# Attention front of a fused kernel: transposes by token halves, mixing by column halves, three runs of one TensorE tiling a step

## The chip, the cores and the metric

One Trainium2 chip, of which one NeuronCore is used. The metric is the device time of one execution in microseconds (us); lower is better. Three runs of the kernel before gave a median of 671.93 us (670.54 to 672.46).

## The reference, cut to what matters

Block-wise linear attention with decay feeds a mixer. With B = 4 batches, H = 8 heads, S = 768 tokens, 64 elements a head, C = 512 channels:

```python
for b in range(S // 64):                        # attention, per head
    qb, kb, vb = q[:, :, sl], k[:, :, sl], v[:, :, sl]
    intra = (qb @ kb^T * Dmask) @ vb            # Dmask: powers of lam below the diagonal
    inter = (qb * lam_pow) @ kv_state
    out[:, :, sl] = intra + inter
    kv_state = lam_block * kv_state + (kb * rev_pow)^T @ vb
x = out as (B, S, C)
h = x^T @ U @ V                                 # U: S x 32, V: 32 x S, per batch
u = x + h^T                                     # mixing along the tokens
y = u + relu(u @ w_ch1) @ w_ch2                 # w_ch1: 512 x 2048, w_ch2: 2048 x 512
```

## The kernel before, in words

The tokens of all batches are cut into 24 tiles of 128 tokens (`NS` = 24, six a batch, `NT` = 6). The work has three parts.

The **front** is a loop of 24 steps, whose pieces are written out by hand in the list `pieces` (L562 to L584); each engine does its instructions in the order in which the pieces issue them. Step s has, in this order:

- `prep(s+1)` (L360): the q and k of the next tile, four 128x128 transposes each on TensorE into one PSUM bank each, and a ScalarE copy of each bank (L358) to `qt` and `kt`; then the loads of later q and k are issued on SyncE's queue. `raw_pool` has 3 buffers for q and v, 4 for k.
- `scale(s+1)`: GpSimd multiplies `qt` with powers of lam (`qs`, L383), and k of the tile after that (`ks`, L372).
- `mix(done)` with done = s - 7 (L512): one matmul of a 128x128 block `v_hl` by `p_hl` (128x512) into one bank, and the VectorE addition to the tile `x_nat` (L518).
- `intra(s)` (L446): 16 products of masked scores and v on tiles of 128 rows x 64 columns; ScalarE copies the result from PSUM to `x_nat` (L459).
- `state(s)` (L411): 8 products of k and v on 128x64 tiles, and the VectorE update of `kv` (L426); then the load of a later v. The last tile of a batch (c = 5) has none.
- `turned`: ScalarE and GpSimd finish the split of an earlier u (L551, L552).
- `scores(s+1)` (L394): 8 products of k and q, on 64x128 tiles up to s = 6, and on 64x64 tiles (16 products) from s = 7.
- `inter(s+1)` (L431): 16 products of `qs` and `kv` on 64x64 tiles. The first tile of a batch has none.
- `masked(s+1)` (L405): VectorE multiplies scores and mask, two instructions (L409), into `sm`, which `intra(s+1)` reads.
- `turn(done)` (L523): four 128x128 transposes of the mixed tile on TensorE into one bank, the store of the tile to `u_d` on SyncE's queue (L535), and two VectorE instructions that split it (`ut` L537, `u_hl` L548). It is in the front for the first 16 tiles.

At the first step of a batch `low(b-1)` (L464) gives x^T U for the batch before, on 128x32 tiles, and `low_rows` (L477) splits it into the `p_hl` that `mix` uses; at some steps `aside` puts one or two VectorE instructions of the split of the first two w_ch1 blocks behind `masked` (from s = 12 ahead of it).

The **first product** (`hidden`, L719) is u @ w_ch1, by 128x512 matmuls in FP32R. Its first units have the last eight `turn`, the last `mix` and the last `low` between their matmuls, at places of the list `rest` (L788 to L802). The **second product** (`product`, L857) ends the kernel.

PSUM in the front: six tags, `pq`, `pk`, `pt`, `pu` of one bank and `pss`, `px` of two, one buffer each. `put` uses `pt`, `mix` `pu`, and `state` the bank of `pk`.

Of the kernel before, what the change touches and what calls it, by code (L numbers as in the profile page):

```python
# [14 lines left out]
P = 128  # L15
# [3 lines left out]
def kernel(  # L19
# [319 lines left out]
    def keep_busy(n):  # L339

        out = one_bank([P, C], "idle", "pq")
        for i in range(n):
            nc.tensor.matmul(out=out[:, 0:P], lhsT=blank, rhs=blank, start=True, stop=True)  # L343
# [3 lines left out]
    def turn_half(s, a0, name):  # L347

        ts, tag = (qts, ("pq", "pt")) if name == "q" else (kts, ("pk", "pu"))
        if a0 == 0:  # L350
            ts[s] = att.tile([P, HP, P], FP32, tag=name + "t", bufs=2, name=name + "t")
        n = HP // parts(s)
        pt = one_bank([P, n, P], "p" + name, tag[a0 > 0])
        for a in range(a0, a0 + n):
            nc.tensor.transpose(  # L355
                out=pt[:, a - a0, :], in_=raw[s, name][:, 2 * a : 2 * a + 2, :], identity=ident
            )
        nc.scalar.copy(ts[s][:, a0 : a0 + n, :], pt)  # L358

    def prep(s):  # L360
        for a0 in range(0, HP, HP // parts(s)):
            for name in "qk":
                turn_half(s, a0, name)
        st[s].update(qt=qts.pop(s), kt=kts.pop(s))
        for name in "qk":
            load_next(name)
# [27 lines left out]
    def scores(s):  # L394
        qt, kt = st[s]["qt"], st[s]["kt"]
        st[s]["pss"] = pss = two_banks("pss", "pss").rearrange("p x (a i) -> p x a i", a=HP)
        for a in range(HP):
            for x in range(2):
                for rows in half if s > NT else [slice(0, P)]:
                    nc.tensor.matmul(  # L400
                        out=pss[rows, x, a, :], lhsT=kt[half[x], a, rows],
                        rhs=qt[half[x], a, :], start=True, stop=True,
                    )
# [7 lines left out]
    def state(s):  # L411
        c = s % NT
        if c < NT - 1:
            ks, vr = st[s]["ks"], raw[s, "v"]
            pkv = one_bank([P, HP, D], "pkv", "pk")
# [48 lines left out]
    def low(b):  # L464

        tag = "pq" if b else "pu"
        pp = one_bank([P, P], "pp", tag) if b < B - 1 else bank([P, P], "pp", "b2")
# [7 lines left out]
        pps[b] = pp  # L475

    def low_rows(b):  # L477

        pp, t = pps.pop(b), tmp("p_h")[0:R]
        h, h2, l, l2 = (p_hl[g * R : (g + 1) * R] for g in range(G))  # L480
        own = [(slice(g * R, (g + 1) * R), slice(g * P, (g + 1) * P)) for g in range(G)]
        if b == 0:

            rows_f = tmp("p_f")[0:R]
            for rows, cols in own:
                nc.scalar.copy(rows_f[:, cols], pp[rows])
            own = [(slice(0, R), slice(0, C))]
            pp = rows_f
        for rows, cols in own:
            nc.vector.tensor_scalar(  # L490
                t[:, cols].bitcast(U32), pp[rows].bitcast(U32), HI, None, ALU.bitwise_and
            )

        def low_part():
            for rows, cols in own:
                nc.vector.tensor_tensor(
                    out=l[:, cols], in0=pp[rows], in1=t[:, cols], op=ALU.subtract
                )

        def spread():  # L500
            nc.scalar.copy(h, t)
            nc.scalar.copy(h2, t)

        def spread_low():
            nc.scalar.copy(l2, l.bitcast(FP32))
# [5 lines left out]

    def mix(s):  # L512
        b, c = divmod(s, NT)
        pu = one_bank([P, C], "pu", "pu") if s < NS - NT - 1 else bank([P, C], "pu", "b2")
        nc.tensor.matmul(  # L515
            out=pu, lhsT=v_hl[:, c * P : (c + 1) * P], rhs=p_hl, start=True, stop=True
        )
        nc.vector.tensor_tensor(out=xs[s], in0=pu, in1=xs[s], op=ALU.add)  # L518

    uhl, ud, turned = {}, {}, {}  # L520
    hl_at, d_at = [hl_pool], [d_pool]

    def turn(s):  # L523
# [6 lines left out]
        pt = one_bank([P, CT, P], "put", "pt") if g < FG else bank([P, CT, P], "put", "b1")  # L530
        for ct in range(CT):
            nc.tensor.transpose(  # L532
                out=pt[:, ct, :], in_=xs[s][:, ct * P : (ct + 1) * P], identity=ident
            )
        nc.sync.dma_start(out=u_d[s], in_=xs.pop(s))  # L535
        t = tmp("ut").rearrange("p (c n) -> p c n", n=P)
        nc.vector.tensor_scalar(t.bitcast(U32), pt.bitcast(U32), HI, None, ALU.bitwise_and)  # L537
        hi, low, diff = uhl[g][:, 0, :, cols], uhl[g][:, 1, :, cols], ud[g][:, :, cols]
        if g >= FG:

# [7 lines left out]
        nc.vector.tensor_tensor(out=low, in0=pt, in1=t, op=ALU.subtract)  # L548
# [6 lines left out]

        turned[s] = rest

    pieces = [("prep", 0), ("scale", 0), ("scores", 0), ("inter", 0), ("masked", 0)]  # L562
    for s in range(NS):
# [3 lines left out]
        step = [("prep", s + 1), ("scale", s + 1)] * more + [("fade", s)] * (c == 1)  # L567
        step += [("late", s - 1)] * (s in (NT, 3 * NT - 1))
        step += [("mix", done)] * (0 <= done < NS - NT - 1)
        step += [("low", b - 1)] * (c == 0 and b > 0)  # L570
        step += [("low_rows", b - 1)] * (c == 0 and b > 0)
# [6 lines left out]
        step += [("scores", s + 1)] * more  # L578
        step += [("aside", s)] * (s >= 2 * NT)
        step += [("inter", s + 1), ("masked", s + 1)] * more  # L580
        step += [("fade", s + 1)] * (more and c > 0)
        step += [("aside", s)] * (s < 2 * NT)
        step += [("turn", done)] * (done >= 0 and done // TG < FG)
# [3 lines left out]
    def load_next(name, engine=nc.sync):  # L587
# [7 lines left out]
        "low": low, "low_rows": low_rows, "next_of_low": next_of_low, "mix": mix, "turn": turn,  # L595
        "scale": scale, "turned": lambda s: turned.pop(s)(),
# [80 lines left out]
    make_identity(nc, ident)  # L677
    keep_busy(2)
    pl = one_bank([P, H], "pl", "pt")
# [99 lines left out]
    def run_units(units, side, every=lambda i: None):  # L779
# [10 lines left out]
        (0, 4, "turn", c0 - 2), (0, 6, "mix", c0 - 1), (0, 9, "low", b), (0, 14, "low_rows", b),  # L790
# [179 lines left out]
```

## Time and profile before

| | us |
|---|---|
| median of 3 runs | 671.93 |
| the profiled execution | 671.76 |
| its span, from the first to the last instruction | 669.9 |
| TensorE busy in the span | 663.9 (99%) |
| VectorE / ScalarE / GpSimd busy | 497.5 / 277.5 / 112.1 |
| front, to the start of the first matmul of the first product | 118.98 |

The page gives busy time by engine, the span in 40 slices, and the chain of work that ended last. Below it, groups of instructions by line and shape are a second view, and the timeline (start, length, engine, line, operation, how many) a third. TensorE's records overlap: a matmul's length includes its passage through the array, so a rate is read from starts and not from lengths. An FP32 product shows as two records, a transpose as one. `128*64` ahead of a shape is the tile of the array: rows by columns.

### The profile page before, as it was taken

The page shows a single profiled execution, that of the slowest core. Times are in us where ns is not written, and L with a number is a line of the kernel's source. Part 1 is how long each engine was busy: PE and PEld are TensorE (multiplying, and loading weights), DVE is VectorE, ACT ScalarE, POOL GpSimd, SP SyncE. Part 2 cuts the span into 40 slices and gives each one's busy share as a digit, 9 for nine tenths or more (in the row PEclk, how much of TensorE's full clock was granted, in tenths as well). Part 3 has the DMA queues.
Part 4 walks back from the last instruction along what each step waited for, and adds up shares of the span by engine and source line. Part 5 has one row for each costly group of instructions (what it writes and reads, how often), then busy time and mean ns, then how long its engine had stood idle before and what let it go on. Part 6 is the DMA issues. An engine that isn't in the chain of part 4 may idle for free.

```text
span 669.9 us, 13328 instructions
## 1 busy us (share of the span) xinstructions
PE 663.9 (99%) x5204; PEld 544.5 (81%) x5204; DVE 497.5 (74%) x873; ACT 277.5 (41%) x517; POOL 112.1 (17%) x92
## 2 busy tenths in 40 slices
PE   9999999999999999999999999999999999999997
PEld 8898989788888888888888888888888888888886
DVE  4689989877999777777797265787586775865864
ACT  4675866454655444444454122232322322322320
POOL 4455767240000000000000000030030300300300
PEclk9999999999999999999999999999999999999999
DMA  8999894354776655555577989854363353543421
GB/s 188 219 234 248 212 246 141 102 196 153 262 251 233 215 202 202 201 202 204 204 282 273 326 308 392 282 184 136 95 220 95 118 196 95 160 155 94 163 90 63
DMA packets 131776, 131.29 MB, mean 196 GB/s; under 512 B 81346, under 2 KB 89794, under 8 KB 131714
## 3 DMA queue, kind: packets, MB, share of 16 engines
q1 hardware_dynamic: 130512, 130.05, 61.1%
q8 instruction: 41, 0.67, 0.4%
q10 hardware_dynamic: 1202, 0.39, 0.2%
q14 instruction: 21, 0.17, 0.1%
HBM read 80.09 MB, written 50.33 MB: 195 GB/s over the span
## 4 chain that ended last, share of the span: by engine, by line
PE 97%; DVE 1%; DMA 1%; ACT 0%; issue 0%; DVEq 0%; ACTq 0%
PE pz L733 27%; PE pz L868 13%; PE pz L866 13%; PE pd L743 13%; PE pd L870 13%; PE px L453 4%; PE pss L400 3%; PE put L532 2%; PE pq L355 2%; PE pkv L418 1%; PE pk L355 1%; PE px L441 1%; DMA qraw<-in_q_dram 1%; PE pp L470 1%; PE pu L515 1%; PE idle L343 0%
## 5 line engine op out<-in xcount | busy, mean ns | idle before, releaser
L733 PE MATMUL pz<-u_hl,w 128*128 128x512 f32 x768 | 190.5, 397 | 0.0
L733 PEld LDWEIGHTS pz<-u_hl,w 128*128 128x128 f32 x768 | 144.0, 188 | 35.4 <-issue 0.4
L868 PE MATMUL pz<-w_hl,m 128*128 128x512 f32 x384 | 151.1, 396 | 0.0
L866 PE MATMUL pz<-w_hl,m 128*128 128x512 f32 x384 | 150.9, 396 | 0.0
L870 PE MATMUL pd<-w_d,m 128*128 128x512 f32 x384 | 149.5, 396 | 0.0
L849 ACT ACTIVATE m<-mt 128x512 fp32r<-128x512 f32 x96 | 60.5, 632 | 196.4 <-PE pd L870 140.9
L850 DVE SCALAR_TENSOR_TENSOR m<-rm,m 128x512 fp32r<-128x512 f32 x96 | 71.4, 746 | 53.8 <-ACT m L849 53.5
L895 POOL TENSOR_TENSOR o<-o,u 128x512 f32<-128x512 f32 x20 | 29.9, 1527 | 447.4 <-DVE o L891 447.4
L748 DVE SCALAR_TENSOR_TENSOR r<-pd,r 128x512 f32<-128x512 f32 x96 | 61.8, 686 | 53.6 <-ACT r L739 43.5
L743 PE MATMUL pd<-u_d,w 128*128 128x512 f32 x384 | 98.6, 397 | 0.0
L739 ACT ACTIVATE r<-pz 128x512 f32<-128x512 f32 x96 | 52.2, 596 | 93.2 <-PE pz L733 92.5
L868 PEld LDWEIGHTS pz<-w_hl,m 128*128 128x128 f32 x384 | 72.3, 188 | 17.7
L870 PEld LDWEIGHTS pd<-w_d,m 128*128 128x128 f32 x384 | 72.3, 188 | 17.6
L866 PEld LDWEIGHTS pz<-w_hl,m 128*128 128x128 f32 x384 | 72.3, 188 | 17.6
L743 PEld LDWEIGHTS pd<-u_d,w 128*128 128x128 f32 x384 | 72.1, 188 | 17.3
L851 DVE SCALAR_TENSOR_TENSOR m<-m 128x512 fp32r<-128x512 f32 x96 | 69.1, 721 | 0.9
L848 DVE TENSOR_SCALAR mt<-rm 128x512 uint32<-128x512 uint32 x96 | 46.1, 481 | 26.4 <-DMA rm<-r_d 26.1
L409 DVE TENSOR_TENSOR sm<-pss,mask 128x512 f32<-128x512 f32 x48 | 30.9, 685 | 7.3 <-PE pss L400 7.1
L212 ACT CAST w<-wt 128x512 fp32r<-128x512 f32 x32 | 19.9, 620 | 30.6 <-DVE wt L209 23.4
L383 POOL TENSOR_TENSOR qs<-qt,powq 128x512 f32<-128x512 f32 x20 | 25.9, 1297 | 20.3 <-ACT qt L358 19.8
L453 PEld LDWEIGHTS px<-vraw,sm 128*64 128x64 f32 x768 | 24.6, 137 | 5.5 <-issue 2.3
L453 PE MATMUL px<-vraw,sm 128*64 128x64 f32 x768 | 28.1, 225 | 0.1
(88 smaller groups left out, 682.1 us busy)
## 6 DMA issues: line engine op xcount, KB each, us to landing
r_d<-r SPq DMA_DIRECT2D x96, 256.0 KB, 2.4
rm<-r_d SPq DMA_DIRECT2D x96, 256.0 KB, 2.7
words<-in_moe_w_ch_dram SPq DMA_DIRECT2D x30, 512.0 KB, 4.5
w_d<-w SPq DMA_DIRECT2D x16, 768.0 KB, 3.3
w_hl<-w_d SPq DMA_DIRECT2D x16, 512.0 KB, 6.3
vraw<-in_v_dram SPq DMA_DIRECT2D x24, 256.0 KB, 5.0
u_d<-x_nat SPq DMA_DIRECT2D x24, 256.0 KB, 3.7
u<-u_d SPq DMA_DIRECT2D x24, 256.0 KB, 4.0
```

The costliest lines, as they stand in the source:

```text
L453: nc.tensor.matmul(out=px[half[t], x, a, :], lhsT=sm[:, x, a, half[t]], rhs=vr[:, 2 * a + x, :], start=(first and a == 0), stop=(a == HP - 1),
L733: nc.tensor.matmul(out=acc[g][0], lhsT=w[:, n, ct, :], rhs=uhl[g][:, n, ct, :], start=(ct == 0 and n == 0), stop=(ct == CT - 1 and n == 1),)
L739: nc.scalar.mul(rs[g], acc[g][0], 4096.0 + 1.0)
L743: nc.tensor.matmul(out=acc[g][1], lhsT=w[:, 2, ct, :], rhs=ud[g][:, ct, :], start=(ct == 0), stop=(ct == CT - 1),)
L748: nc.vector.scalar_tensor_tensor(rs[g], acc[g][1], 4096.0, rs[g], ALU.mult, ALU.add)
L848: nc.vector.tensor_scalar(t.bitcast(U32), r.bitcast(U32), HI, None, ALU.bitwise_and)
L849: nc.scalar.activation(out=m[:, 0], in_=t, func=AF.Relu)
L850: nc.vector.scalar_tensor_tensor(m[:, 1], r, 0.0, hi, ALU.max, ALU.subtract)
L851: nc.vector.scalar_tensor_tensor(m[:, 2], hi, E, low, ALU.mult, ALU.subtract)
L866: nc.tensor.matmul(out=pz, lhsT=m[:, 0, cols], rhs=hl[:, 0], start=first, stop=False)
L868: nc.tensor.matmul(out=pz, lhsT=m[:, 1, cols], rhs=hl[:, 1], start=False, stop=end)
L870: nc.tensor.matmul(out=pd, lhsT=m[:, 2, cols], rhs=dd, start=first, stop=end)
```

## The change

The six tags become four of two banks each: `pm`, `pss`, `pqk`, `px`. q and k are transposed together into `pqk` by halves of the tokens: 16 transposes of 64 rows to 128x64, each half to a bank of its own. `turn` does the same with 8 transposes into the first half of `pm`'s banks, and `mix` computes halves of the columns with 64 of the 128 rows each, in 4 matmuls of 128x256, into the second half of these banks. `state` takes a bank of `pqk`, `low` one of `px`. Scores are on 64x64 tiles from the second tile on.

In a step the order is now `prep(s+1)`, `turn(done-1)`, `mix(done)`, then `intra(s)` and `state(s)`, then `scores(s+1)` and `inter(s+1)`. The VectorE instructions of `turn` and `mix` are pieces of their own (`split`, `mixed`), ahead of `intra`; the store of the tile is one too, at the end of the step. `low(b)` stands at the end of a batch's last step, and ScalarE copies its result from PSUM. `mix` of tile 17 moves from the first product to step 23. As the changed program's waits stand, the copies of q and k both wait for the last transpose of k, and `split` waits for the last matmul of `mix`.

```diff
@@ -338,29 +338,36 @@
 
     def keep_busy(n):
 
-        out = one_bank([P, C], "idle", "pq")
+        out = two_banks("idle", "pm")[:, 0]
         for i in range(n):
             nc.tensor.matmul(out=out[:, 0:P], lhsT=blank, rhs=blank, start=True, stop=True)
 
     qts, kts = {}, {}
 
-    def turn_half(s, a0, name):
-
-        ts, tag = (qts, ("pq", "pt")) if name == "q" else (kts, ("pk", "pu"))
+    def turn_parts(s, a0):
+
+        n = HP // parts(s)
         if a0 == 0:
-            ts[s] = att.tile([P, HP, P], FP32, tag=name + "t", bufs=2, name=name + "t")
-        n = HP // parts(s)
-        pt = one_bank([P, n, P], "p" + name, tag[a0 > 0])
-        for a in range(a0, a0 + n):
-            nc.tensor.transpose(
-                out=pt[:, a - a0, :], in_=raw[s, name][:, 2 * a : 2 * a + 2, :], identity=ident
-            )
-        nc.scalar.copy(ts[s][:, a0 : a0 + n, :], pt)
+            for ts, name in ((qts, "qt"), (kts, "kt")):
+                ts[s] = att.tile([P, HP, P], FP32, tag=name, bufs=2, name=name)
+        pt = two_banks("pqk", "px" if a0 else "pqk")[:, :, 0 : 2 * n * D]
+        pt = pt.rearrange("p t (n a i) -> p t n a i", n=2, a=n)
+        for i, name in enumerate("qk"):
+            for a in range(n):
+                for t in range(2):
+                    nc.tensor.transpose(
+                        out=pt[:, t, i, a, :],
+                        in_=raw[s, name][half[t], 2 * (a0 + a) : 2 * (a0 + a) + 2, :],
+                        identity=ident[half[t], half[t]],
+                    )
+        for i, ts in enumerate((qts, kts)):
+            nc.scalar.copy(
+                ts[s][:, a0 : a0 + n, :].rearrange("p a (t i) -> p t a i", t=2), pt[:, :, i]
+            )
 
     def prep(s):
         for a0 in range(0, HP, HP // parts(s)):
-            for name in "qk":
-                turn_half(s, a0, name)
+            turn_parts(s, a0)
         st[s].update(qt=qts.pop(s), kt=kts.pop(s))
         for name in "qk":
             load_next(name)
@@ -396,7 +403,7 @@
         st[s]["pss"] = pss = two_banks("pss", "pss").rearrange("p x (a i) -> p x a i", a=HP)
         for a in range(HP):
             for x in range(2):
-                for rows in half if s > NT else [slice(0, P)]:
+                for rows in half if s > 0 else [slice(0, P)]:
                     nc.tensor.matmul(
                         out=pss[rows, x, a, :], lhsT=kt[half[x], a, rows],
                         rhs=qt[half[x], a, :], start=True, stop=True,
@@ -412,7 +419,7 @@
         c = s % NT
         if c < NT - 1:
             ks, vr = st[s]["ks"], raw[s, "v"]
-            pkv = one_bank([P, HP, D], "pkv", "pk")
+            pkv = two_banks("pkv", "pqk")[:, 0, 0 : HP * D].rearrange("p (a e) -> p a e", a=HP)
             for a in range(HP):
                 for x in range(2):
                     nc.tensor.matmul(
@@ -463,8 +470,7 @@
 
     def low(b):
 
-        tag = "pq" if b else "pu"
-        pp = one_bank([P, P], "pp", tag) if b < B - 1 else bank([P, P], "pp", "b2")
+        pp = two_banks("pp", "px")[:, 0, 0:P] if b < B - 1 else bank([P, P], "pp", "b2")
         for c in range(NT):
             for g in range(G):
                 nc.tensor.matmul(
@@ -472,53 +478,100 @@
                     rhs=xs[b * NT + c][:, g * P : (g + 1) * P],
                     start=(c == 0), stop=(c == NT - 1),
                 )
-        pps[b] = pp
+        if b == B - 1:
+            pps[b] = pp
+            return
+        pps[b] = rows_f = tmp("p_f")[0:R]
+        for g in range(G):
+            nc.scalar.copy(rows_f[:, g * P : (g + 1) * P], pp[g * R : (g + 1) * R])
 
     def low_rows(b):
...
+        rows_f = pp
+        nc.vector.tensor_scalar(t.bitcast(U32), rows_f.bitcast(U32), HI, None, ALU.bitwise_and)
+        wide = [slice(x * 2 * P, (x + 1) * 2 * P) for x in range(2)]
+
+        def place(g, low):
+            return p_hl[g * R : (g + 1) * R, wide[low]]
+
+        def spread():
+            for g in range(G):
+                nc.scalar.copy(place(g, 0), t[:, wide[g // 2]])
...
     def next_of_low(b):
         pps[b].pop(0)()
 
+    pms = {}
+
+    def both_halves(s):
+        if s not in pms:
+            pms[s] = two_banks("pm", "pqk" if s == NS - NT - 1 else "pm")
+        return pms[s]
+
     def mix(s):
         b, c = divmod(s, NT)
-        pu = one_bank([P, C], "pu", "pu") if s < NS - NT - 1 else bank([P, C], "pu", "b2")
-        nc.tensor.matmul(
-            out=pu, lhsT=v_hl[:, c * P : (c + 1) * P], rhs=p_hl, start=True, stop=True
-        )
+        weights = v_hl[:, c * P : (c + 1) * P]
+        if b < B - 1:
+            pm = both_halves(s)[:, :, 2 * P :]
+            for low in range(2):
+                for x in range(2):
+                    nc.tensor.matmul(
+                        out=pm[:, x], lhsT=weights[half[x]],
+                        rhs=p_hl[half[x], low * 2 * P : (low + 1) * 2 * P],
+                        start=(low == 0), stop=(low == 1),
+                    )
+            return
+        pu = bank([P, C], "pu", "b2")
+        nc.tensor.matmul(out=pu, lhsT=weights, rhs=p_hl, start=True, stop=True)
         nc.vector.tensor_tensor(out=xs[s], in0=pu, in1=xs[s], op=ALU.add)
+
+    def mixed(s):
+        pm, x = pms.pop(s)[:, :, 2 * P :], xs[s].rearrange("p (x e) -> p x e", x=2)
+        nc.vector.tensor_tensor(out=x, in0=pm, in1=x, op=ALU.add)
 
     uhl, ud, turned = {}, {}, {}
     hl_at, d_at = [hl_pool], [d_pool]
+
+    def store(s):
+        nc.sync.dma_start(out=u_d[s], in_=xs[s])
 
     def turn(s):
 
@@ -527,16 +580,17 @@
             uhl[g] = hl_at[g >= FG].tile([P, 2, CT, N], F32R, tag="hl", name="u_hl")
             ud[g] = d_at[g >= FG].tile([P, CT, N], F32R, tag="d", name="u_d")
         cols = slice(n * P, (n + 1) * P)
-        pt = one_bank([P, CT, P], "put", "pt") if g < FG else bank([P, CT, P], "put", "b1")
-        for ct in range(CT):
-            nc.tensor.transpose(
-                out=pt[:, ct, :], in_=xs[s][:, ct * P : (ct + 1) * P], identity=ident
-            )
-        nc.sync.dma_start(out=u_d[s], in_=xs.pop(s))
-        t = tmp("ut").rearrange("p (c n) -> p c n", n=P)
-        nc.vector.tensor_scalar(t.bitcast(U32), pt.bitcast(U32), HI, None, ALU.bitwise_and)
         hi, low, diff = uhl[g][:, 0, :, cols], uhl[g][:, 1, :, cols], ud[g][:, :, cols]
         if g >= FG:
+            pt = bank([P, CT, P], "put", "b1")
+            for ct in range(CT):
+                nc.tensor.transpose(
+                    out=pt[:, ct, :], in_=xs[s][:, ct * P : (ct + 1) * P], identity=ident
+                )
+            store(s)
+            del xs[s]
+            t = tmp("ut").rearrange("p (c n) -> p c n", n=P)
+            nc.vector.tensor_scalar(t.bitcast(U32), pt.bitcast(U32), HI, None, ALU.bitwise_and)
 
             nc.vector.scalar_tensor_tensor(diff, t, 1.0 + E, pt, ALU.mult, ALU.subtract)
             uf = tmp("uf").rearrange("p (c n) -> p c n", n=P)
@@ -545,7 +599,14 @@
             nc.gpsimd.tensor_tensor(out=low, in0=uf, in1=t, op=ALU.subtract)
             return
 
-        nc.vector.tensor_tensor(out=low, in0=pt, in1=t, op=ALU.subtract)
+        pt = both_halves(s + 1)[:, :, 0 : 2 * P].rearrange("p t (c i) -> p t c i", i=D)
+        for ct in range(CT):
+            for n in range(2):
+                nc.tensor.transpose(
+                    out=pt[:, n, ct, :], in_=xs[s][half[n], ct * P : (ct + 1) * P],
+                    identity=ident[half[n], half[n]],
+                )
+        del xs[s]
 
         def rest():
             nc.scalar.mul(hi, t, E)
@@ -553,22 +614,37 @@
                 out=diff, in0=hi.bitcast(FP32), in1=low.bitcast(FP32), op=ALU.subtract
             )
 
+        def parts_of(what):
+            return what.rearrange("p c (t i) -> p t c i", t=2)
+
+        t = tmp("ut").rearrange("p (c n) -> p c n", n=P)
+        split_t = parts_of(t.bitcast(U32))
         turned[s] = rest
 
-
-
-
+        def split():
+            nc.vector.tensor_scalar(split_t, pt.bitcast(U32), HI, None, ALU.bitwise_and)
+            nc.vector.tensor_tensor(
+                out=parts_of(low), in0=pt, in1=parts_of(t), op=ALU.subtract
+            )
+
+        splits[s] = split
+
+    splits = {}
 
     pieces = [("prep", 0), ("scale", 0), ("scores", 0), ("inter", 0), ("masked", 0)]
     for s in range(NS):
         b, c = divmod(s, NT)
         done = s - NT - 1
         more = s + 1 < NS
-        step = [("prep", s + 1), ("scale", s + 1)] * more + [("fade", s)] * (c == 1)
+        turns = done > 0 and (done - 1) // TG < FG
+        mixes = 0 <= done < NS - NT - 1
+        step = [("prep", s + 1), ("scale", s + 1)] * more
+        step += [("turn", done - 1)] * turns + [("mix", done)] * mixes
+        step += [("mix", done + 1)] * (not more)
+        step += [("fade", s)] * (c == 1)
         step += [("late", s - 1)] * (s in (NT, 3 * NT - 1))
-        step += [("mix", done)] * (0 <= done < NS - NT - 1)
-        step += [("low", b - 1)] * (c == 0 and b > 0)
-        step += [("low_rows", b - 1)] * (c == 0 and b > 0)
+        step += [("split", done - 1)] * turns + [("mixed", done)] * mixes
+        step += [("mixed", done + 1)] * (not more)
         step += [("intra", s)]
         step += [("next_of_low", b - 1)] * (c == 0 and b > 0)
         step += [("late", s)] * (s < NT - 1 or s == NT) + [("state", s)]
@@ -576,11 +652,13 @@
         step += [("turned", done - 1)] * (done > 0) + [("late", s)] * (done >= 0)
         step += [("next_of_low", b - 1)] * (c == 0 and b > 0)
         step += [("scores", s + 1)] * more
+        step += [("low", b)] * (more and c == NT - 1)
         step += [("aside", s)] * (s >= 2 * NT)
         step += [("inter", s + 1), ("masked", s + 1)] * more
+        step += [("low_rows", b)] * (more and c == NT - 1)
         step += [("fade", s + 1)] * (more and c > 0)
         step += [("aside", s)] * (s < 2 * NT)
-        step += [("turn", done)] * (done >= 0 and done // TG < FG)
+        step += [("store", done)] * (done >= 0 and done // TG < FG)
         pieces += step
     waiting = {name: list(range(NS)) for name in "qkv"}
 
@@ -593,6 +671,7 @@
         "prep": prep, "fade": fade, "scores": scores, "masked": masked, "inter": inter,
         "intra": intra, "state": state,
         "low": low, "low_rows": low_rows, "next_of_low": next_of_low, "mix": mix, "turn": turn,
+        "mixed": mixed, "store": store, "split": lambda s: splits.pop(s)(),
         "scale": scale, "turned": lambda s: turned.pop(s)(),
     }
     def v_steps():
@@ -675,8 +754,8 @@
     for name in "qkv":
         load_next(name)
     make_identity(nc, ident)
+    pl = two_banks("pl", "pss")[:, 0, 0:H]
     keep_busy(2)
-    pl = one_bank([P, H], "pl", "pt")
     nc.tensor.matmul(out=pl, lhsT=lam_row[:, H:], rhs=lam_row[:, 0:H], start=True, stop=True)
     keep_busy(3)
     nc.vector.tensor_copy(out=lamb, in_=pl)
@@ -787,7 +866,7 @@
     c0, b = NS - NT, B - 1
     rest = [
         (0, 4, "enter", None),
-        (0, 4, "turn", c0 - 2), (0, 6, "mix", c0 - 1), (0, 9, "low", b), (0, 14, "low_rows", b),
+        (0, 7, "turn", c0 - 2), (0, 9, "low", b), (0, 14, "low_rows", b),
         (0, 14, "next_of_low", b), (0, 14, "next_of_low", b), (0, 14, "next_of_low", b),
         (0, 18, "turn", c0 - 1), (0, 22, "mix", c0),
     ]
```

## Prediction

> **What bounds the kernel now.** I read the page first: the span and the chain of work that ended last.
>
> ```profile
> span 669.9 us, 13328 instructions
> ...
> PE 97%; DVE 1%; DMA 1%; ACT 0%; issue 0%; DVEq 0%; ACTq 0%
> ```
>
> TensorE (PE) is the chain. The change touches only the front, so next comes the timeline of TensorE in one of its steps.
>
> ```profile
> 48.35 0.66 PE L532 MATMUL put<-ident,x_nat 128*128 128x128 f32 x4
> 48.84 0.60 PE L355 MATMUL pq<-ident,qraw 128*128 128x128 f32 x4
> 49.28 0.60 PE L355 MATMUL pk<-ident,kraw 128*128 128x128 f32 x4
> 49.63 0.47 PE L515 MATMUL pu<-vp 128*128 128x512 f32 x1
> 50.04 1.15 PE L453 MATMUL px<-vraw,sm 128*64 128x64 f32 x32
> 51.02 0.64 PE L418 MATMUL pkv<-vraw,ks 128*64 128x64 f32 x16
> 51.59 1.10 PE L400 MATMUL pss<-qt,kt 64*64 64x128 f32 x32
> 52.51 0.64 PE L441 MATMUL px<-kv,qs 64*64 64x64 f32 x32
> ```
>
> Starts count here. The next step begins at 53.09, so a step is 4.74 us with no idle time in it: 12 transposes and the mix take 1.69 (48.35 to 50.04), intra 0.98, state 0.57, scores 0.92, inter 0.58. The tiling (the number pair ahead of the shape) changes three times. VectorE in the same step:
>
> ```profile
> 49.91 0.68 DVE L537 TENSOR_SCALAR ut<-put 128x512 uint32<-128x512 uint32 x1
> 50.62 0.69 DVE L548 TENSOR_TENSOR u_hl<-put,ut 128x512 fp32r<-128x512 f32 x1
> 51.23 0.68 DVE L518 TENSOR_TENSOR x_nat<-pu,x_nat 128x512 f32<-128x512 f32 x1
> 51.82 0.41 DVE L426 TENSOR_TENSOR kv<-pkv,faded 128x256 f32<-128x256 f32 x1
> 52.76 1.29 DVE L409 TENSOR_TENSOR sm<-pss,mask 128x512 f32<-128x512 f32 x2 [0.52 <-PE pss L400]
> ```
>
> From start to start ut costs 0.71, u_hl 0.61, x_nat 0.60, kv 0.35, sm 0.60 each: 3.5 us, and 0.4 to 0.8 of `aside`. VectorE is close behind TensorE. Last, SyncE's queue:
>
> ```profile
> 76.81 0.74 SPq L535 DMA_DIRECT2D u_d<-x_nat  x1
> 77.64 0.38 SPq L279 DMA_DIRECT2D qraw<-in_q_dram  x1
> 78.12 0.63 SPq L279 DMA_DIRECT2D kraw<-in_k_dram  x1
> 78.85 3.22 SPq L279 DMA_DIRECT2D vraw<-in_v_dram  x1
> 82.17 0.73 SPq L535 DMA_DIRECT2D u_d<-x_nat  x1
> ```
>
> The issues follow each other within 0.1 us, from 8 to 100 us, and the DMA share in steps of the front is 0.74 to 0.97. The buffer that the load at 78.85 fills (v of tile 17) was free when tile 14's state ended at 76.6, so the 3.22 us are no wait for TensorE: the queue runs at its own pace. **Loads and stores are a second bound that a faster TensorE does not move.**
>
> **What the Trainium skill says.** "TensorEngine Tiling (Array Packing)", Key Properties: a change of the tiling mode drains TensorE. The trace agrees: from the last transpose's start to the next tiling's first record it is 0.203 us where 0.109 is the pace, so about 0.09 a change. "TensorE: Matmul & The Clock Gate", Part 3: matmuls of different row groups run at once. The early scores agree: two 64x128 records start 7 ns apart, and each pair takes 0.109 like one 128x128 record. The same page, LDWEIGHTS: a load costs its columns divided by 1.2 GHz, 107 ns for 128, whatever the rows. For a transpose the trace differs: the first two loads of `put` start 57 ns apart (87.77 and 87.83). "PSUM — Partial Sum Buffer", bank collisions: no two engines on one bank and quadrant at a time. That fits the new waits: q's copy behind k's transposes, `split` behind the mix, as these share banks.
>
> **The change, part by part.**
>
> *Transposes.* A 128x128 transpose takes 0.109 (48.84 to 49.28 is four). In halves 64 columns stream instead of 128, and two row tiles run together: a pair should take what a pair of 128x64 records takes in intra, 0.058. The weight load of 0.057 fits under it. Unknown: such a transpose is not in the trace. Its bounds are 0.058 and 0.109 a pair (the page's 107 ns, or no concurrency); below 0.058 no row goes. I take 0.058. Twelve pairs, of which eleven intervals lie ahead of the mix: 11 x 0.051 = 0.56 us a step.
>
> *Mix.* Before: one matmul of 512 columns. After: two pairs of 256 columns, the same columns streamed, if FP32R keeps its rate at 256. I take 0; from -0.03 to +0.2 a step.
>
> *Changes of tiling.* Three before, three after: 0. Scores of steps with s up to 6 take 1.09 (15.44 to 16.53) on 64x128 tiles and 0.92 on 64x64: 0.16 saved in each early step, whose transposes save 8 x 0.051 = 0.41. Together 0.57.
>
> *The new wait on VectorE.* Let the transposes start at 0. The last pair starts at 0.70 (0.055 first load, 11 x 0.058), the last mix record about 0.92, intra at 1.13, and inter would start at 1.13 + 0.98 + 0.57 + 0.92 = 3.60. `split` can start 0.41 after the last mix record (0.31 of passage, 0.1 to the waiting engine, as kv starts 0.1 after pkv's end): 1.33. Behind it on VectorE stand ut 0.71, u_hl 0.61, x_nat 0.60, kv 0.42, and 0.06 to TensorE: kv is ready at 3.73, and inter, which reads it, waits 0.13. Before, ut followed `put`, which came first in the step, and had this time. Bounds: 0 (an earlier release) to 0.3. Queued behind the wait are kv and masked; masked starts after scores at 3.9, ends its second half at 5.1, and the next intra wants it at 5.5, so it is no later bound; with an `aside` of 0.6 ahead of it, 5.4, still in time.
>
> A full step is then 4.74 - 0.56 + 0.13 = 4.31: 0.43 saved. ScalarE's copies of q and k end at 1.9, ahead of state (2.1) which reuses their bank; GpSimd's qs ends at 2.7, ahead of 3.6. Its three instructions are 3.6 us.
>
> *The queue's cap.* A tile's v landed before it was read by: tile 4 0.2 us (26.86, intra at 27.07), tile 7 1.6 (38.79, 40.43), tile 17 4.65 (issue at 78.85, landing 6.0 later at 84.8, intra at 89.46). The store of tile 6 landed at 82.3, and ScalarE writes over its buffer at 85.9: 3.65, and 0.7 more before TensorE feels it. TensorE can be ahead by these amounts and no more, since the stores and loads keep their order and nothing of them is shortened. Early steps: 0.57 each from tile 4, capped at 1.6 by tile 7. Then ten steps of 0.43 would give 5.9 at tile 17; the cap leaves 4.65. After it the queue pulls away (tile 18 has 5.9, tile 21 6.5), and five full steps add 2.15: 6.8.
>
> *Moved pieces.* `mix` of tile 17 leaves the first product (0.235 saved there) and enters the last front step (0.22), which saves 0.2 of transposes. `low` keeps its 1.25 us; before, TensorE stood about 0.6 ahead of `put` at 61.7 for a late `x_nat`, and `turn` now comes a step after `mix`; against it the copies of `low`'s result, 4 x 0.26 on ScalarE, lie ahead of q's. I set these against each other, and keep +-0.5. Sum: 6.8 + 0.2 = 7.0 us. The first product follows at TensorE's pace, so all of it arrives at the end.
>
> The profiled execution's span goes from 669.9 to 662.9, its time (1.9 us more) from 671.76 to 664.8. The median is 0.2 above it: 664.9.
>
> **Rivals.**
>
> *Part of the gain (chance 0.12).* A pair at 0.080 instead of 0.058, or waits of 0.3 a step at inter and on ScalarE: about 0.2 a step over 15 steps and 1 us of the early ones, 4 us: 668. For it: VectorE is 88% to 98% busy in the steps from 68 us (4.18 to 4.76 of 4.7). Against: the sum above leaves 0.1 to 0.4 of slack.
>
> *The transposes do not get shorter (0.10).* Bound by the load of 128 columns, 0.109 a pair. Left are the early scores, at most 0.16 x 5 = 0.8, and the new wait, 0.13 x 14 = 1.8: +1.0, 672.9. For it: the page's price, and the first two loads of the early FP32 scores (128 columns) do start 0.109 apart. Against: the 57 ns of a transpose's load.
>
> *VectorE becomes the bound (0.08), slower.* Its three reads ut, u_hl and x_nat now have pieces of 64 elements and two banks, and stand between mix and kv. A step is the way from the last mix record over these to inter (2.81) and on through inter and the next transposes (1.5). Each 0.1 more on each read lengthens it by 0.3. With what early steps gain, it decides from 0.18 more each; at 0.3 more (0.9 instead of 0.6) a step is 5.2 us, +0.47 over 14 steps less 1.6: +5, 676.9. Against: ScalarE reads `px` in pieces of 64 over two banks in 0.58, like its plain reads (0.57).
>
> **How the numbers follow.** The forecast has 0.70. Its own range: a front 4.5 to 9.9 us shorter, by a wait of 0.3 to none and a cap that moves a microsecond or two: 662.0 to 667.4. A range for 8 in 10 takes in the partial gain: 661.9 to 670.0. A measurement tells 0.3% (2 us) from no change; faster by more is the forecast and the partial gain, 0.82; within it the unshortened transposes, 0.10; slower 0.08.
>
> **What would show it.** Right: 16 transposes of q and k in about 0.9 us, pairs 0.058 apart; the step 4.2 to 4.4 us; the idle time ahead of inter on kv about 0.1; stalls ahead of intra on v's landing near tiles 3, 4, 7 and 16 to 17; landings where they were; the first product starting near 112. Wrong: pairs at 0.109; ut, u_hl or x_nat longer than 0.75; or v landing earlier than before, which lifts the cap and with it the gain.

## The result and the profile after

The change makes the kernel slower by 0.7%. Times are medians; the last two columns are from the one profiled execution of each kernel. The last one sums the pauses of TensorE, each over 0.1 us, that no wait in the profile explains and that lie at the packet boundaries described below.

| kernel | us | ratio to before (95%) | first product starts | TensorE idle without a wait, front |
|---|---|---|---|---|
| before | 672.19 (670.54 to 672.46) | | 118.99 | 0 |
| after | 676.55 (676.29 to 677.47) | 1.0072 (1.0053 to 1.0092) | 125.01 | 7.2 |

The whole loss is in the front: 6.0 us at the start of the first product, 5.8 on the span (the profiled execution is the slowest of the four after, with a mean granted clock of 0.997 where the other three have 1.000, so it shows 1.4 us more than the medians). The page after, span and chain:

```profile
span 675.7 us, 14142 instructions
...
PE 96%; issue 1%; DVE 1%; DMA 1%; ACT 0%; ACTq 0%; DVEq 0%
```

TensorE is still the chain, yet 1% is now "issue": time in which it waited for nothing that the profile shows. Its timeline (start, length, engine, line, how many, idle time ahead) in a late step of the front, to lay beside the step of before:

```profile
102.97 0.40 PE L358 MATMUL pqk<-ident,qraw 64*128 64x64 f32 x6
104.08 0.28 PE L358 MATMUL pqk<-ident,qraw 64*128 64x64 f32 x2 [0.71 <-issue]
104.14 0.47 PE L358 MATMUL pqk<-ident,kraw 64*128 64x64 f32 x8
...
105.08 1.15 PE L460 MATMUL px<-vraw,sm 128*64 128x64 f32 x32
106.07 0.64 PE L425 MATMUL pkv<-vraw,ks 128*64 128x64 f32 x16
106.63 1.10 PE L407 MATMUL pss<-qt,kt 64*64 64x128 f32 x32
107.68 0.59 PE L448 MATMUL px<-kv,qs 64*64 64x64 f32 x25
109.05 0.34 PE L448 MATMUL px<-kv,qs 64*64 64x64 f32 x7 [0.78 <-issue]
```

Six transposes of q run, then TensorE stands for 0.71 us in the middle of eight like instructions, whose data are all there; then 25 of 32 products of inter, and 0.78 us. Intra (0.99) and state (0.56) are what they were. The two gaps are 127 matmul records apart. There are twelve gaps of this kind, 7.2 us in all, and none has a wait. Counted in recorded instructions of TensorE (matmuls, weight loads and semaphore instructions), all twelve are a multiple of 256 apart, within one.

VectorE's three reads of PSUM, which a rival of the prediction had longer (the two numbers behind the bar are busy time in us and mean ns of one, from 40 us on), after:

```profile
L625 DVE TENSOR_SCALAR ut<-pm 128x512 uint32<-128x512 uint32 x15 | 10.3, 686 | 5.3 <-PE pm L556 5.2
L568 DVE TENSOR_TENSOR x_nat<-pm,x_nat 128x512 f32<-128x512 f32 x15 | 10.2, 680 | 0.0
L626 DVE TENSOR_TENSOR u_hl<-pm,ut 128x512 fp32r<-128x512 f32 x14 | 9.7, 691 | 0.5
```

And before:

```profile
L537 DVE TENSOR_SCALAR ut<-put 128x512 uint32<-128x512 uint32 x15 | 10.2, 681 | 0.0
L518 DVE TENSOR_TENSOR x_nat<-pu,x_nat 128x512 f32<-128x512 f32 x16 | 10.9, 681 | 0.0
L548 DVE TENSOR_TENSOR u_hl<-put,ut 128x512 fp32r<-128x512 f32 x15 | 10.4, 692 | 0.5
```

They are unchanged. SyncE's queue, around the load of tile 17's v, which is the second line:

```profile
80.27 0.52 SPq L279 DMA_DIRECT2D kraw<-in_k_dram  x1
81.35 0.61 SPq L279 DMA_DIRECT2D vraw<-in_v_dram  x1
82.06 0.76 SPq L574 DMA_DIRECT2D u_d<-x_nat  x1
83.25 0.37 SPq L279 DMA_DIRECT2D qraw<-in_q_dram  x1
83.72 1.59 SPq L279 DMA_DIRECT2D kraw<-in_k_dram  x1
86.55 0.37 SPq L279 DMA_DIRECT2D vraw<-in_v_dram  x1
```

This load lands at 86.04, and intra reads it at 93.82: 7.8 us in hand (before 4.65). The queue even has pauses now (85.31 to 86.55). It waits for TensorE, and not TensorE for it.

**What ends a gap.** The page has a queue of its own for instructions; before and after:

```profile
q8 instruction: 41, 0.67, 0.4%
```

```profile
q8 instruction: 44, 0.72, 0.5%
```

0.72 MB in 44 packets is 16.4 KB each; over 5610 matmuls and 5610 weight loads it is 64 bytes an instruction, so a packet holds 256 instructions: 126 matmuls, 126 loads and a few others. Below, such a set of 256 is called a piece. Packets of this queue in the trace of after, beside the first record of the piece that they bring (us):

| packet | first record | gap ahead | record after packet's end |
|---|---|---|---|
| 50.01 to 50.97 | 52.34 | 1.94 | 1.4 |
| 74.66 to 75.60 | 76.95 | 0.83 | 1.4 |
| 96.92 to 97.86 | 99.19 | 0.48 | 1.3 |
| 101.80 to 102.67 | 104.08 | 0.71 | 1.4 |
| 106.57 to 107.45 | 109.05 | 0.78 | 1.6 |

At all twelve gaps TensorE resumes 1.26 to 1.60 us after the end of a packet. Before, packets ended mostly 1.7 to 3.1 us ahead of their first record. So the **theory**: TensorE runs short of instructions, as their supply is late. A full step has 140 matmul records now (before 125), to be issued in less time. "Runtime: NRT & Kernel Launch", Instruction fetch mechanics, of the Trainium skill describes refills in blocks of 256 instructions, fetched while the block before runs, and holds them mostly hidden. The trace agrees on the block, and not on the hiding: 7.2 us of gaps.

**Rivals**: VectorE's new wait, or loads that land too late, hold the step, and the gaps are only how the trace shows it. The next runs tell these apart.

### The profile page after: what moved, and what is told of

It reads as the page before. It is cut to its first block, busy times and chain, and to the rows that moved or that the text cites. A ratio compares the mean times of both kernels' runs of the same rounds, so it can differ in the third digit from the quotient of the medians.

```text
span 675.7 us, 14142 instructions
## 1 busy us (share of the span) xinstructions
PE 661.4 (98%) x5610; PEld 540.5 (80%) x5610; DVE 496.3 (73%) x864; ACT 281.6 (42%) x534; POOL 113.5 (17%) x92
## 4 chain that ended last, share of the span: by engine, by line
PE 96%; issue 1%; DVE 1%; DMA 1%; ACT 0%; ACTq 0%; DVEq 0%
PE pz L812 27%; PE pz L947 13%; PE pz L945 13%; PE pd L822 13%; PE pd L949 13%; PE px L460 4%; PE pss L407 4%; PE pqk L358 2%; PE px L448 2%; PE pkv L425 1%; PE pp L476 1%; PE pm L556 1%; PE pm L605 1%; DMA kraw<-in_k_dram 1%; PE put L587 1%
## 5 line engine op out<-in xcount | busy, mean ns | idle before, releaser
L460 PE MATMUL px<-vraw,sm 128*64 128x64 f32 x768 | 31.4, 228 | 2.8 <-issue 1.7
L460 PEld LDWEIGHTS px<-vraw,sm 128*64 128x64 f32 x768 | 26.3, 138 | 7.5 <-issue 2.4
```

The source lines that it names most:

```text
L460: nc.tensor.matmul(out=px[half[t], x, a, :], lhsT=sm[:, x, a, half[t]], rhs=vr[:, 2 * a + x, :], start=(first and a == 0), stop=(a == HP - 1),
```

## Experiments: more and fewer instructions, idle queues

**Scores on 64x128 tiles throughout** (8 products a step instead of 16, of two records each):

```diff
-                for rows in half if s > 0 else [slice(0, P)]:
+                for rows in [slice(0, P)]:
```

> The changed kernel with its scores on 64x128 tiles in every step: 124 matmul records a full step instead of 140 (an early one 112 instead of 128), each with its weight load, and 0.16 us more array time a step. Supply theory (TensorE gets its instructions in pieces of 256, one in about 4.85 us while the loads run, so 126 records with their loads cannot take less): the gaps inside runs of like records mostly go, a step takes about 4.75, the first product starts at 118 to 120 and the time is 669 to 673, faster than the change. VectorE theory (the new wait and longer reads hold a step): TensorE's own work is 0.16 longer in 22 steps and the time is 676 to 680. Load theory (q, k and v land too late): nothing moves, 676 to 677.

**After and before without most loads** (both leave out the loads of q, k and v of later tiles and compute with other data):

```diff
...
+        bufs = 4 if name == "k" else 3
+        if s >= bufs:
+            raw[s, name] = held[name, s % bufs]
+            return
...
-        raw[s, name] = t
+        raw[s, name] = held[name, s] = t
```

> The changed kernel without the loads of q, k and v after the first three tiles (four of k): later tiles read the buffers of earlier ones again, so the output is that of other data. TensorE's instructions are the same. Supply theory: a piece of instructions comes faster through idle queues, the gaps without a wait go, a full step takes 4.3 to 4.4, the first product starts at 111 to 114 and the time is 662 to 666. VectorE theory: the time stays at 675 to 677. Load theory: 662 to 667 as well, but then the gaps of the change must have been waits for a landing.

> The kernel before without the same loads (output of other data). Supply theory: its 125 records a step are within the supply, so little moves: first product at 117.5 to 119, time 670 to 672; beside the changed kernel without loads this gives what the change is worth where instructions are not short, 5 to 8 us. VectorE theory: the changed kernel without loads is slower than this one by about the 4 us that separate the kernels with loads. Load theory: as the supply theory.

**The kernel before with empty products**, at the head of `inter` (`none` is a tile of zeros):

```diff
...
+        if s > 0:
+            for i in range(16):
+                x, t = divmod(i % 4, 2)
+                nc.tensor.matmul(
+                    out=both[half[t], x, N - 1 : N], lhsT=none[half[x], half[t]],
+                    rhs=none[half[x], 0:1], start=True, stop=True,
+                )
```

> The kernel before with 16 empty products a step more (bf16, one column, on 64x64 tiles just ahead of inter, into an unused column): 141 matmul records a step with their loads. At inter's pace (32 records in 0.58 us) they are at most 0.29 us of work a step, 6.7 us over 23 steps. Supply theory: a full step grows to 141/126 x 4.85 = 5.4 while the loads run, early ones to about 4.6; gaps without a wait appear in the middle of runs, 126 records apart, and the time rises by 8 to 13 us, to 680 to 685. VectorE and load theories: no such gaps, and a rise of 2 to 7 us, 674 to 679.

| kernel | us | ratio to before (95%) | first product starts | idle without a wait |
|---|---|---|---|---|
| after, wide scores | 671.55 | 0.9981 (0.9970 to 0.9993) | 120.32 | 1.5 |
| after, no loads | 669.02 | 0.9941 (0.9921 to 0.9962) | 117.44 | 0.6 |
| before, no loads | 670.82 | 0.9978 (0.9965 to 0.9990) | 117.80 | 0 |
| before, 16 more | 677.00 | 1.0058 (1.0037 to 1.0079) | 123.34 | 0.4 |

Each set of experiments ran beside the kernel before, whose medians were 672.87 in this set, 671.59 in the second and 671.87 in the third. The ratios take this out; times of different sets can be off against each other by about 1 us.

Wide scores: more work for TensorE, fewer instructions, and 5 us less than after (6 by the ratios). Neither rival allows that. No loads: the same instructions, and the gaps are nearly gone (0.6 us left). The share of the DMA engines that the data queue takes between 10 and 110 us, after without loads, and after (9 to 109 us):

```profile
q1 hardware_dynamic: 7044, 5.87, 18.7%
```

```profile
q1 hardware_dynamic: 70827, 21.53, 88.7%
```

What did not come as expected tells more. Sixteen more products cost 4.1 us and not 8 to 13: undisturbed steps took 4.89 us, with 141 records and no gap. So the theory's fixed rate, a piece in 4.85 us, is wrong: here 126 records in 4.37 us were mostly served. The supply is a **latency**: in after, a packet starts 1.2 to 2.6 us (at the two worst gaps 3.4 and 3.6) after TensorE has begun the piece before, takes 0.9 to 1.5, and its first record runs at least 1.26 later. A gap comes where this is longer than the time in which TensorE spends 126 records, and that is 3.96 at the change's pace of 4.4 a step. The traces also show which part the loads lengthen. In the median a packet starts 2.0 us into the piece before with loads and 1.2 without, while the packet itself takes 0.96 and 0.99.

The change without loads gained 1.8 us on its partner, not 5 to 8, as its expectation had it: something else is missing from the forecast too (below).

**The threshold itself**: `range(32)` in place of `range(16)`.

> The kernel before with 32 empty products a step instead of 16: 157 records a full step. The first 16 made an undisturbed full step 0.15 us longer (4.74 to 4.89), so these make it 5.04, and 126 records then take 4.05 us as in the changed kernel, where 16 had left 4.37. Supply theory, as it now stands (a piece of instructions is asked for when TensorE begins the one before it, and needs 0.5 to 2.5 us in a queue, 0.9 to 1.5 of transfer and at least 1.3 to the first instruction, in sum 3.7 to 4.9): gaps without a wait as in the changed kernel, 0.2 to 0.8 at most boundaries, about 5 us, and the time is 683 to 688. If the gaps belong to something else in the change, only the work is added, 0.15 a step, 3.5 us on the 677.0 with 16: 680 to 681.

682.56 us, ratio 1.0155 (1.0134 to 1.0177), with no part of the change in it. A step is 5.11, so 126 records take 4.10, and the gaps are there, 3.2 us without a wait (16 more had 0.4), again in the middle of runs:

```profile
61.42 0.42 PE L439 MATMUL px<-none 64*64 64x1 bf16 x32
61.75 0.47 PE L449 MATMUL px<-kv,qs 64*64 64x64 f32 x17
63.50 0.46 PE L449 MATMUL px<-kv,qs 64*64 64x64 f32 x15 [1.28 <-issue]
```

It lies just under the range expected: the work grew by 0.22 a step instead of 0.15, but the gaps by 2.7 us instead of about 5, and the kernel before was 1.3 us faster in this set. The mechanism is shown on both kernels. Over the traces of all thirteen kernels of this document there are 58 such gaps in the front; they end 1.23 to 1.67 us after the end of a packet, and no piece begins less than 1.2 us after its packet. How many gaps there are depends on more than the rate.

## Experiments: why the change gains little even without gaps

Times from the start of one intra to a later one, in us, from the traces (undisturbed: without a gap):

| tiles (all of them counted) | before, no loads | after, no loads | after |
|---|---|---|---|
| 0 to 4 (early) | 21.76 | 21.36 | 22.07 |
| one early step, undisturbed | 4.29 | 4.05 | 4.05 |
| 5 and 6 (first end of a batch) | 9.09 | 10.38 | 10.68 |
| one full step, undisturbed | 4.74 | 4.42 | 4.53 |
| 11 and 12 (second end) | 10.80 | 10.03 | 10.03 |
| 17 and 18 (third end) | 10.13 | 10.53 | 11.27 |

A full step of after without loads:

```profile
74.04 1.15 PE L464 MATMUL px<-vraw,sm 128*64 128x64 f32 x32
75.02 0.64 PE L429 MATMUL pkv<-vraw,ks 128*64 128x64 f32 x16
75.59 1.20 PE L411 MATMUL pss<-qt,kt 64*64 64x128 f32 x32
76.65 0.69 PE L452 MATMUL px<-kv,qs 64*64 64x64 f32 x32
77.27 0.46 PE L362 MATMUL pqk<-ident,qraw 64*128 64x64 f32 x8
77.57 0.41 PE L362 MATMUL pqk<-ident,kraw 64*128 64x64 f32 x8
77.82 0.41 PE L609 MATMUL pm<-ident,x_nat 64*128 64x64 f32 x8
78.05 0.48 PE L560 MATMUL pm<-vp 64*128 64x256 f32 x4
78.46 0.73 PE L464 MATMUL px<-vraw,sm 128*64 128x64 f32 x14
```

Transposes and mix take 1.19 (77.27 to 78.46) instead of 1.69: the shorter transposes are real. From scores to inter it is 1.06 instead of 0.92; `kv` ends on VectorE at 76.50:

```profile
76.08 0.42 DVE L437 TENSOR_TENSOR kv<-pkv,faded 128x256 f32<-128x256 f32 x1
```

So inter waits 0.14 on VectorE, the wait that was forecast with 0.13.

The early steps fell from 4.29 to 4.05 only. My first idea was the way from scores over the mask to intra. So this run multiplies only half of it:

```diff
...
+            n = HP if s == 0 else HP // 2
             nc.vector.tensor_tensor(
-                out=sm[:, x], in0=pss[:, x], in1=mask[:, x], op=ALU.mult
+                out=sm[:, x, 0:n], in0=pss[:, x, 0:n], in1=mask[:, x, 0:n], op=ALU.mult
             )
```

> The changed kernel without loads, and with the mask multiplied into half of the scores' columns only (two VectorE instructions of 256 elements instead of 512; the other half keeps the first tile's values, so the output is of other data). TensorE's instructions are the same. Latency theory (an early step is the way from scores over both halves of sm to intra, and the shorter transposes only leave TensorE waiting there): early steps go from 4.05 to 3.7 to 3.8, full ones from 4.41 to about 4.35, the time from 669.0 to 665.5 to 667.5. If TensorE's own work or its supply sets the early steps, they stay at 4.05 and the time at 668.5 to 669.5.

667.17 us, in the range that the idea gave, but 1.3 of the gain comes from an earlier start in the profile (intra of tile 0 at 8.84 against 10.16); the early steps stayed at 4.05 and the full ones at 4.42. As the only cause the idea fell. The products of state in three early steps of this kernel, what they waited for:

```profile
its engine sat idle before it (us, times) until:
  PE pkv L434: 4.4, 3
  ACT kt L368: 0.8, 3
```

(The first line is VectorE, which reads the tile; the second counts weight loads as well as products, 0.14 us each.) State takes a bank of `pqk` and cannot start before ScalarE has copied k out of it: at 23.09 the copy ends, at 23.15 state starts, 0.14 after intra left TensorE free. With the full mask (after without loads) intra takes 1.30 instead of 0.98 (23.20 to 24.50), as the second half of `sm` ends at 23.52, and the copy of k ends at 24.44, just ahead of state. So two chains of the same length hold the early step; the runs with both taken away are below.

The first end of a batch, after without loads:

```profile
35.60 0.42 PE L362 MATMUL pqk<-ident,kraw 64*128 64x64 f32 x8
36.55 1.15 PE L464 MATMUL px<-vraw,sm 128*64 128x64 f32 x32 [0.54 <-ACT p_f L490]
...
39.68 0.69 PE L452 MATMUL px<-kv,qs 64*64 64x64 f32 x32 [0.26 <-DVE kv L435]
...
40.83 1.14 PE L560 MATMUL pm<-vp 64*128 64x256 f32 x4
41.90 0.28 PE L464 MATMUL px<-vraw,sm 128*64 128x64 f32 x2
```

Intra of tile 6 needs the bank in which `low` left its result, and waits for ScalarE's four copies; inter waits for `kv`; the first mix takes 1.07 instead of 0.42, as its `p_hl` is late. In all these waits are about 1.5 us.

## Experiments: taking these waits away

**`low` of batch 0 in a bank of `pm`, `aside` ahead of `low_rows`**, with 64x64 and with 64x128 scores:

```diff
-        pp = two_banks("pp", "px")[:, 0, 0:P] if b < B - 1 else bank([P, P], "pp", "b2")
+        pp = two_banks("pp", "px" if b else "pm")[:, 0, 0:P] if b < B - 1 else bank([P, P], "pp", "b2")
...
+        step += [("aside", s)] * (s == NT - 1)
         step += [("low_rows", b)] * (more and c == NT - 1)
...
-        step += [("aside", s)] * (s < 2 * NT)
+        step += [("aside", s)] * (s < 2 * NT and s != NT - 1)
```

> The changed kernel with low of the first batch in the bank of pm instead of px, and the VectorE instructions of aside ahead of low_rows in that step. The wait of 0.54 us ahead of intra of tile 6 (ScalarE's four copies of low's result) and the 0.26 on kv go, and the first mix waits less for p_hl. If these waits are a loss of their own: 0.8 to 1.4 us, 675.1 to 675.8. If the supply of instructions sets the pace there too: under 0.5, 676 to 676.7.

> The same edit on the changed kernel with 64x128 scores in every step, which had 671.6. There the supply is short in fewer places, so more of the 0.8 to 1.4 us should show: 670.2 to 671. If it beats the kernel before by more than its interval, it is faster than both.

| kernel | us | ratio to before (95%) | first product starts | idle without a wait |
|---|---|---|---|---|
| after, low moved | 674.99 | 1.0044 (1.0026 to 1.0061) | 122.54 | 5.3 |
| wide, low moved | 670.51 | 0.9981 (0.9971 to 0.9990) | 119.42 | 1.3 |

The first is 1.6 us faster than after, but the intervals of the two ratios overlap, and tiles 5 and 6 take 10.42 instead of 10.68, only 0.26 of it: the 0.54 at intra is gone, and state then waits 0.35. The rest fits the gaps, 5.3 us instead of 7.2. The second has the ratio of its parent: no gain shown. Its trace has one more pause without a wait, 0.60 at 39.05, that lies at no packet boundary and is not counted. Five other kernels have one of 0.2 to 0.35 near the same place, the 0.35 just named among them; the profile does not show what ends them.

**Two more edits on top of these**, for the two chains of the early steps. State's result goes to a bank that needs no copy of k, and intra takes all products of the first half of `sm` first:

```diff
-            pkv = two_banks("pkv", "pqk")[:, 0, 0 : HP * D]
+            pkv = two_banks("pkv", "pqk" if s > NT else "pm")[:, 0, 0 : HP * D]
...
-        for a in range(HP):
-            for x in range(2):
+        for x in range(2):
+            for a in range(HP):
```

> The kernel with low's bank and aside moved (675.0) and two edits more that take waits from the early steps: state's result up to tile 6 in a bank of pm, so that it does not wait for ScalarE's copy of k, and intra takes all products of the first half of sm before those of the second. In the early steps both chains were 4.05 us long; TensorE's own work is 3.7. Supply theory: 126 records cannot come faster than about 4 us, early steps stay at 4.0 to 4.8 with gaps in the middle of runs, and the gain is under 0.8: 674.2 to 675. Without a limit of supply: 0.35 in five steps, 673.2.

> The same two edits on the version with 64x128 scores (670.5): 112 records in an early step, whose work is then 3.9 us, so that 126 records take 4.4. Early steps go from 4.3 to 3.9 to 4.1 where the supply holds, about 1 to 1.5 us in all: 669 to 669.5, faster than the kernel before by about 0.4%. If early steps stay at 4.3, a third chain holds them, and it is 670.5.

> As the one before, with the addition of mix to x_nat behind the update of kv on VectorE. On 64x128 scores inter begins 0.16 us later than on 64x64, so kv is in time already: no change against it, within 0.5 us.

| kernel | us | ratio to before (95%) | first product starts | idle without a wait |
|---|---|---|---|---|
| after, freed | 676.38 | 1.0065 (1.0045 to 1.0086) | 123.74 | 7.6 |
| wide, freed | 669.47 | 0.9963 (0.9946 to 0.9980) | 117.19 | 0.7 |
| wide, freed, mix's addition later | 672.35 | 1.0009 (0.9997 to 1.0020) | 122.34 | 1.8 |

On 64x64 scores the edits give nothing, less even than was expected with a short supply: up to tile 6 alone there are four gaps of 0.58 to 0.82, 126, 127 and 253 matmul records apart:

```profile
14.87 0.22 PE L460 MATMUL px<-vraw,sm 128*64 128x64 f32 x1 [0.80 <-issue]
19.59 0.27 PE L460 MATMUL px<-vraw,sm 128*64 128x64 f32 x1 [0.82 <-issue]
24.08 0.28 PE L460 MATMUL px<-vraw,sm 128*64 128x64 f32 x3 [0.58 <-issue]
32.90 0.45 PE L460 MATMUL px<-vraw,sm 128*64 128x64 f32 x7 [0.72 <-issue]
```

Where waits go, the supply takes their place. On 64x128 scores early steps fall from 4.34 to between 3.91 and 4.08, undisturbed full ones are 4.45, and this version is faster than both kernels: by 0.4% than before, as expected, and by about 1% than after. The third, with the addition of `mix` behind `kv` on VectorE, was to change nothing and lost 2.9 us. Its VectorE:

```profile
83.18 0.69 DVE L626 TENSOR_TENSOR u_hl<-pm,ut 128x512 fp32r<-128x512 f32 x1
84.40 0.42 DVE L433 TENSOR_TENSOR kv<-pkv,faded 128x256 f32<-128x256 f32 x1 [0.54 <-PE pkv L425]
84.75 0.68 DVE L568 TENSOR_TENSOR x_nat<-pm,x_nat 128x512 f32<-128x512 f32 x1
```

The addition had filled the time until state was done; behind `kv` it leaves VectorE idle for 0.54 and comes ahead of the mask, for which intra then waits three times:

```profile
87.54 0.69 PE L460 MATMUL px<-vraw,sm 128*64 128x64 f32 x16 [0.34 <-DVE sm L416]
...
116.40 1.28 PE L460 MATMUL px<-vraw,sm 128*64 128x64 f32 x32 [0.35 <-DVE sm L416]
...
121.13 1.05 PE L460 MATMUL px<-vraw,sm 128*64 128x64 f32 x24 [0.34 <-DVE sm L416]
```

These three waits (1.0 us together) and a gap of 1.41 at 33.06 are 2.4 us, less than half of the 5.2 us by which the first product starts later in this profile (674.86 us, above the median of 672.35). The rest is not explained here.

## Why the prediction was wrong, point by point

- *What bounds the kernel.* TensorE, as said. But its busy time was taken for work of the array; the page's instruction queue was not read.
- *Transposes*, 0.56 saved a step: right in the main. 1.69 became 1.19, so 0.50 is saved; pairs come 0.057 to 0.075 apart.
- *Mix* and *changes of tiling*, 0: right within 0.1 together.
- *The new wait on VectorE*, 0.13: right, 0.14 without loads.
- *"A full step is then 4.74 - 0.56 + 0.13 = 4.31"*: this is the step that failed. As work it holds to 0.1 (4.42 without loads). As the time of a step it lacks a term: whether 140 records with their weight loads can be supplied in it. With the data loads the steps of tiles 8 to 21 took 4.5 to 7.0 us; the gaps are 7.2 us in all, and without data loads 0.6. Supply is not the whole miss: without the gaps the change gains 1.8 us where 7.0 were forecast. The next two points hold the larger part of that.
- *Early steps*, 0.57 saved each: 0.24. TensorE's own saving was counted, and the copies of k ahead of state and the mask ahead of intra, which the long transposes had covered, were not looked at there; the copies' slack was worked out for a full step only.
- *Moved pieces*, 0 with +-0.5: mis-sized. Tiles 5 and 6 lose 1.3 without loads, where 0.57 and 0.43 were to be saved; tiles 17 and 18 lose 0.4 where 0.86 was to be saved; the step of tile 22 goes from 3.87 to 4.27. Only tiles 11 and 12 save 0.8, as forecast.
- *The queue's cap*: not put to the test, as TensorE came later than before and the queue had pauses.
- *The rival with VectorE as the bound* named 676.9, which is near the result by luck: its reason fails, as the three reads are as long as before.
- The granted clock was half, 0.50, from 53.9 to 57.3 us (0.89 and 0.77 in the mean of 50 to 55 and 55 to 60). With a step of 5.80 this is about 1.3 us of the profiled execution. It follows the longest gap (1.94), but gaps of 1.28 to 1.44 in four other kernels left the clock at 1.00, and the freed kernel on 64x64 scores had 0.50 from 42.5 to 45.9 us after no gap over 0.3 in the 9 us before. Its cause stays open.

The difference between after with and without loads is 7.6 us at the first product (8.7 from the start of intra of tile 0): 6.6 of gaps and 1.3 of clock account for most of it. Why a packet in after starts sometimes 1.2 and sometimes 3.5 us into the piece before was not separated. Idle queues bring it earlier and remove nearly all gaps; which property of the loads does it was not tried.

## What to carry to other kernels

Before splitting matmuls into smaller tiles, count instructions as well as columns: divide TensorE's records and weight loads by the step's time, and look in the trace how long before its first record each packet of the instruction queue ends. If that margin is near its minimum (1.2 to 1.3 us here), a faster array buys gaps; a form with fewer, larger instructions can win though it takes longer in the array (124 records in 4.45 us against 140 in 4.42). And work out the slack of every short step apart: long instructions on the bound engine cover waits of others, which come out as soon as they shrink.

## What the runs showed of the hardware that was not expected

- TensorE's instructions come in 16 KB packets of 256 through a queue that the profile lists beside the data queue, as a share of the same 16 DMA engines. The first record of a piece ran 1.2 us or more after the packet's end. With the data queue at 89% of the engines, at a pace of 126 records with their loads in 3.96 us, 12 of 24 pieces came late; with it at 90% and a pace of 4.37 us, 1 of 24; with it at 19% and a pace of about 4, 2 of 24, and single pieces were served in 3.74 us.
- An FP32 transpose of 64 rows on a 64x128 tile is fast: eight records in 0.23 to 0.30 us.
- An empty bf16 product of one column with its load costs TensorE 9 to 12 ns (16 of them 0.15 us a step, 32 of them 0.37).
